# Fewer, larger first transfers: two row tiles of x at once, and eight k tiles of w_in in four pieces

## The chip, the cores and the metric

The kernel runs on one core of one Trainium2 chip. The metric is the device time of one execution in microseconds (us). The time given for a kernel is the median of several runs; details come from one profiled execution. The core's engines work side by side, each through its own list of instructions in order: TensorE (PE: matrix products, with PEld for its weight loads), VectorE (DVE), ScalarE (ACT), GpSimd (POOL), and SyncE (SP), which here issues every transfer. The transfers themselves are carried out by 16 DMA engines.

## What is computed

Two branches work on the same 2048 x 1024 input x, and a gate per row mixes them. Cut to what matters:

```python
def reference(A_x, A_wqkv, A_wo, B_x, B_w_in, B_w_sp, B_b_sp, B_w_out, gate_w):
    # a: attention, 32 heads of 32, each row looks at 8 rows (itself and 7 before, 2 apart)
    qkv = x @ wqkv; logits = q . k[idx] * Dh ** -0.5; o = softmax(logits) . v[idx]; a = o @ wo
    # b: a gated MLP with mixing over rows
    z = gelu(x @ w_in)                      # 2048 x 3584
    z1, z2 = z[:, :1792], layernorm(z[:, 1792:])
    b = (z1 * (w_sp @ z2 + b_sp)) @ w_out
    g = sigmoid((x * gate_w).sum(-1))
    return g * a + (1 - g) * b
```

x is the same tensor in both branches. All tensors are bf16; products add up in float32.

## The kernel before

Rows of x are cut into 16 row tiles of 128, and its 1024 columns into 8 k tiles of 128. Every product over x runs over the 8 k tiles, with 128 x 128 weights held in the array and up to 512 columns streamed past them. The product's time is set by the columns.

All data in the fast memory lie in one tile, `arena`, and the names are views of it: `xn` (two row tiles of x as they are stored, rows on partitions), `xT` (x transposed, k on partitions, which the products need), `w2` (the second half of w_in, by k tile, plus a column for the gate), `wg_slots` (weights of q, k and v), `z2`, and others. The profile calls all of them `arena`; `ps`, `pt` and `pw` are accumulator tiles.

The order of work is written by hand (`manual_schedule`, L393). TensorE's stages, in order:

1. `warm_up(6)` (L412): six products of zeros (L91), which wait for no transfer.
2. `z2_quad()` (L413): the first two row tiles, columns 0 to 1023 of the second half of w_in. Row tiles 0 and 1 come in untransposed as `xn`, and TensorE transposes them (16 instructions, L238). VectorE (L242) and ScalarE (L244) copy the results to `xT`, two k tiles an instruction. Then 32 products of 512 columns (L223) run with the k tile as the outer loop: for each k tile two row tiles times two column blocks, into four accumulators. So each k tile of w_in is needed for four products before the next one is needed.
3. Row tiles 2 to 15, columns 0 to 511 (`z2_tile(i, 0)`, L417). Their part of `xT` comes from transposing transfers (L403), one per row tile.
4. q, k and v, eight groups of heads (L431), while VectorE does the attention; then the rest of z2 (L452), z1 (L473), the mixing over rows (L487) and the output (L509, L513).

The edit lies in the transfers that SP issues for stages 1 and 2. In the order of its list: the two row tiles of x (L396), the eight k tiles of w_in, 128 x 1024 elements or 256 KB each (L398), the fourteen transposes of x (L403) with weights of the first head group in between (L198), and further weights.

A transfer's end is told by a counter. There are eight counters, used in turn, so a transfer may only be issued when the one eight before it has ended. In the compiled list before, transfers 1 to 8 wait for nothing; the seventh and eighth k tile (transfers 9 and 10) wait for the two x tiles, and the first transpose (transfer 11) waits for k tile 0 (transfer 3).

TensorE waits in the quad as follows: the first transpose of each row tile for that row tile's transfer, and the first product of each k tile for that k tile's transfer.

Of the kernel before, what the change touches and what calls it, by code (L numbers as in the profile page):

```python
# [16 lines left out]
KT = D // P  # L17
# [8 lines left out]
FH = 1792  # L26
NF = FH // P
ZC = 512
# [22 lines left out]
def kernel(  # L51
# [24 lines left out]
    def reg(off, n):  # L76
        return arena[:, off:off + n]
# [43 lines left out]
    xn = reg(A_OFF, 2 * D).rearrange("p (i d) -> p i d", i=2)  # L121
# [13 lines left out]
    w2 = reg(CD_OFF, KT * W2P).rearrange("p (k c) -> p k c", k=KT)  # L135
# [12 lines left out]
    x_v = x2.rearrange("(i q) d -> q i d", q=P)  # L148
# [3 lines left out]
    win_v = B_w_in.rearrange("(k p) c -> p k c", p=P)  # L152
    wsp_v = B_w_sp.rearrange("(a t) s -> a t s", t=P)
    wo_v = A_wo.rearrange("(g h d) n -> g h d n", g=NG, h=HG, d=DH)
    sync = nc.sync
# [236 lines left out]

    tc_order = ctx.enter_context(tc.manual_schedule())  # L393

    for i in range(2):
        sync.dma_start(xn[:, i, :], x_v[:, i, :])  # L396
    for kt in range(KT):
        sync.dma_start(w2[:, kt, 0:2 * ZC], win_v[:, kt, FH:FH + 2 * ZC])  # L398
    for i in range(2, 16):
        if i == 14:  # L400
            load_w(0, 3)
# [173 lines left out]
```

## Time and profile before

| | us |
|---|---|
| median of three runs | 716.58 (715.78 to 716.62) |
| the profiled execution | 716.54 |
| its span, first to last instruction | 714.7 |
| TensorE busy | 706.6 |
| VectorE busy | 414.0 |
| ScalarE busy | 251.3 |
| first product of the quad starts | 6.05 |

The span is what the profile covers; 1.8 us of the execution lie outside it. Busy times overlap, since the engines work side by side. The granted TensorE clock is 0.999 of full speed over the span. In the timeline a line gives the start, the duration or the stretch over which such instructions follow one another, the engine, the line of the kernel, what is written and read, how many, and in brackets the idle time before the first of them with what ended it. A transfer's line under SPq shows the time that SP takes to issue it, not the time that it takes.

### The profile page before, as it was taken

How to read it: one execution, taken by the hardware profiler on the slowest of the kernel's cores; microseconds unless marked ns; L12 is line 12 of the kernel's file. 1: busy time of each engine (PE TensorE's matmuls, PEld its weight loads, DVE VectorE, ACT ScalarE, POOL GpSimd, SP SyncE). 2: the span in 40 equal slices, each digit the busy share in tenths (PEclk: the TensorE clock that was granted, in tenths of full speed). 3: DMA queues.
4: the chain of work that ended last, by engine and by line, in shares of the span. 5: the costliest groups of instructions: out<-in, count | busy, mean ns of one | idle time of the engine just before them, and what ended most of it. 6: DMA issues, size and time to landing. Idle time of an engine off the chain costs nothing.

```text
span 714.7 us, 8897 instructions
## 1 busy us (share of the span) xinstructions
PE 706.6 (99%) x3577; PEld 402.0 (56%) x3628; DVE 414.0 (58%) x429; ACT 251.3 (35%) x483; POOL 11.0 (2%) x23
## 2 busy tenths in 40 slices
PE   8999999999999999999999999999999999999998
PEld 4488888888865554444444444444444444444444
DVE  0000989999999999999997999211222112221111
ACT  4444454445379894353521211111111111121111
POOL 1000000000000102000000000000000000000000
PEclk9999999999999999999999999999999999999999
DMA  9967776667781206954569580772400213002310
GB/s 238 191 149 220 165 200 170 167 133 193 202 237 66 85 1 181 253 184 137 173 196 293 213 174 2 220 146 59 133 1 0 55 49 119 1 1 59 60 45 29
DMA packets 176761, 92.93 MB, mean 130 GB/s; under 512 B 145104, under 2 KB 166992, under 8 KB 176208
## 3 DMA queue, kind: packets, MB, share of 16 engines
q1 hardware_dynamic: 176720, 92.36, 48.9%
q8 instruction: 28, 0.46, 0.3%
q14 instruction: 13, 0.11, 0.0%
HBM read 47.71 MB, written 28.38 MB: 106 GB/s over the span
## 4 chain that ended last, share of the span: by engine, by line
PE 98%; DMA 1%; issue 0%; SPq 0%; DVE 0%; DVEq 0%
PE ps L487 27%; PE ps L431 23%; PE ps L223 14%; PE ps L473 13%; PE psb L513 13%; PE psa L509 8%; DMA arena<-in_B_w_in_dram 1%; SPq L396 0%; DVE arena L517 0%; DVEq L517 0%
## 5 line engine op out<-in xcount | busy, mean ns | idle before, releaser
L487 PE MATMUL ps<-arena 128*128 128x512 bf16 x877 | 192.9, 379 | 1.0
L431 PE MATMUL ps<-arena 128*128 128x384 bf16 x1024 | 166.6, 326 | 0.0
L431 PEld LDWEIGHTS <-arena 128*128 128x128 bf16 x1024 | 147.6, 144 | 18.9
L487 PEld LDWEIGHTS <-arena 128*128 128x128 bf16 x896 | 87.7, 98 | 105.7
L513 PE MATMUL psb<-arena 128*128 128x512 bf16 (+1 forms) x455 | 101.3, 372 | 0.3
L223 PE MATMUL ps<-arena 128*128 128x512 bf16 (+1 forms) x501 | 96.7, 352 | 1.8 <-DMA arena<-in_B_w_in_dram 1.2
L517 DVE SCALAR_TENSOR_TENSOR arena<-psb,omg,arena 128x512 bf16<-128x512 f32 (+1 forms) x33 | 24.3, 735 | 125.4 <-PE psb L513 113.4
L473 PE MATMUL ps<-arena 128*128 128x512 bf16 x439 | 96.4, 379 | 0.5
L266 DVE TENSOR_TENSOR arena<-arena 128x8192 bf16<-128x8192 bf16 x16 | 70.8, 4423 | 43.1 <-DMA arena<-k_d 42.8
L434 ACT CAST arena<-ps 128x384 bf16<-128x384 f32 x128 | 60.5, 480 | 90.2 <-PE ps L431 87.2
L491 ACT CAST arena<-ps 128x512 bf16<-128x512 f32 x56 | 32.8, 586 | 163.4 <-PE ps L487 136.9
L269 DVE TENSOR_TENSOR arena<-arena 128x4096 bf16<-128x4096 bf16 (+1 forms) x64 | 77.7, 1214 | 1.9
L223 PEld LDWEIGHTS <-arena 128*128 128x128 bf16 x512 | 50.1, 98 | 48.0 <-issue 1.3
L513 PEld LDWEIGHTS <-arena 128*128 128x128 bf16 x462 | 45.2, 98 | 51.5
L473 PEld LDWEIGHTS <-arena 128*128 128x128 bf16 x448 | 43.9, 98 | 52.6
L299 DVE TENSOR_TENSOR arena<-arena,att_A 128x8192 bf16<-128x8192 bf16 x16 | 70.7, 4422 | 0.2
L492 DVE TENSOR_TENSOR arena<-arena 128x512 bf16<-128x512 bf16 x56 | 23.6, 422 | 77.9 <-ACT arena L491 77.9
L516 ACT ACTIVATE arena<-psa,g_s 128x512 f32<-128x512 f32 (+1 forms) x33 | 22.2, 674 | 122.3 <-PE psa L509 118.2
L509 PE MATMUL psa<-arena 128*128 128x512 bf16 (+1 forms) x259 | 60.2, 372 | 0.4
L475 ACT ACTIVATE arena<-ps 128x512 bf16<-128x512 f32 x56 | 33.1, 596 | 55.5 <-PE ps L473 49.3
L509 PEld LDWEIGHTS <-arena 128*128 128x128 bf16 x264 | 25.8, 98 | 29.7
L228 ACT ACTIVATE arena<-ps 128x512 bf16<-128x512 f32 (+1 forms) x64 | 34.2, 538 | 23.4 <-PE ps L223 22.1
(54 smaller groups left out, 254.0 us busy)
## 6 DMA issues: line engine op xcount, KB each, us to landing
arena<-k_d SPq DMA_DIRECT2D x8, 960.0 KB, 6.8
arena<-v_d SPq DMA_DIRECT2D x8, 960.0 KB, 5.4
z_d<-arena SPq DMA_DIRECT2D x14, 512.0 KB, 3.3
arena<-z_d SPq DMA_DIRECT2D x4, 1792.0 KB, 7.5
arena<-in_A_wqkv_dram SPq DMA_DIRECT2D x24, 256.0 KB, 4.6
arena<-in_B_w_in_dram SPq DMA_DIRECT2D x4, 1024.0 KB, 7.2
q_d<-arena SPq DMA_DIRECT2D x32, 128.0 KB, 2.1
k_d<-arena SPq DMA_DIRECT2D x32, 128.0 KB, 2.2
```

What stands on the lines that cost most here:

```text
L223: nc.tensor.matmul(ps[:, 0:N], xT[:, kt, i * P:(i + 1) * P], w2[:, kt, ZC * c:ZC * c + N], start=(kt == 0), stop=(kt == KT - 1))
L228: nc.scalar.activation(z2[:, i, ZC * c:ZC * c + n], ps[:, 0:n], ACT.Gelu_apprx_tanh, accum_out=s1[:, 4 * i + c:4 * i + c + 1])
L266: TT(prod.rearrange("p (w j c) -> p w j c", w=W, j=8, c=C), in0, in1, ALU.mult)
L269: return lambda: TT(pv[:, :, 0:half], pv[:, :, 0:half], pv[:, :, half:2 * half], ALU.add)
L299: TT(prod.rearrange("p (w j d h) -> p w j d h", w=W, j=8, d=DH, h=HG), in0, in1, ALU.mult)
L431: nc.tensor.matmul(ps[:, 0:3 * C].rearrange("p (t c) -> p t c", t=3), lhsT, wgt[:, 0:3, kt, :], start=(kt == 0), stop=(kt == KT - 1))
L434: nc.scalar.copy(st[:, j % 4, :], ps[:, 0:3 * C])
L473: nc.tensor.matmul(ps[:], w1[:, kt, (f % 4) * P:(f % 4 + 1) * P], xT[:, kt, 512 * c:512 * (c + 1)], start=(kt == 0), stop=(kt == KT - 1))
L475: nc.scalar.activation(z1s[:, c, :], ps[:], ACT.Gelu_apprx_tanh)
L487: nc.tensor.matmul(ps[:], z2[:, i, f * P:(f + 1) * P], wsp[:, i, :, :].rearrange("p a t -> p (a t)"), start=(i == 0), stop=(i == 15))
L509: nc.tensor.matmul(psa[:, 0:nw], oT[:, kt, :], wo_sb[:, kt, n0:n0 + nw], start=(kt == 0), stop=(kt == KT - 1))
L513: nc.tensor.matmul(psb[:, 0:nw], z1c[:, f, aa * P:(aa + 1) * P], w_out_sb[:, f, n0:n0 + nw], start=(f == 0), stop=(f == NF - 1))
```

## The change

The two row tiles of x become one transfer of 512 KB. The eight transfers of w_in's k tiles become four: k tile 0 (256 KB), k tiles 1 and 2 (512 KB), 3 and 4 (512 KB), and 5 to 7 (768 KB). The bytes, their places and the order in which they are asked for stay the same.

```diff
-    for i in range(2):
-        sync.dma_start(xn[:, i, :], x_v[:, i, :])
-    for kt in range(KT):
-        sync.dma_start(w2[:, kt, 0:2 * ZC], win_v[:, kt, FH:FH + 2 * ZC])
+    sync.dma_start(xn, x_v[:, 0:2, :])
+    for k0, k1 in ((0, 1), (1, 3), (3, 5), (5, 8)):
+        sync.dma_start(w2[:, k0:k1, 0:2 * ZC], win_v[:, k0:k1, FH:FH + 2 * ZC])
     for i in range(2, 16):
         if i == 14:
             load_w(0, 3)
```

In the compiled lists, the instructions of TensorE, VectorE, ScalarE and GpSimd are the same as before and in the same order. SP's list has five transfers fewer at its head. The transposes of row tiles 0 and 1 now wait for the one transfer of x. Products wait at k tiles 0, 1, 3 and 5. With five transfers ahead of them, the first three transposing transfers wait for no counter, and the fourth waits for x. All later lines of the program stand one line higher than before.

## The prediction

> **What bounds the kernel now.** I read the page first: busy time by engine, and the chain that ended last.
>
> ```profile
> span 714.7 us, 8897 instructions
> PE 706.6 (99%) x3577; PEld 402.0 (56%) x3628; DVE 414.0 (58%) x429; ACT 251.3 (35%) x483; POOL 11.0 (2%) x23
> PE 98%; DMA 1%; issue 0%; SPq 0%; DVE 0%; DVEq 0%
> ```
>
> TensorE is busy for 99% of the span and is 98% of the chain. It works through one fixed order, so whatever moves the start of its steady work moves the end by as much. The 1% that is DMA is what the edit touches. The chain of waits, cut to 0 to 40 us, says where that lies (start, length, what):
>
> ```profile
> 0.74 0.39 SPq L396
> 1.18 0.42 SPq L396
> 1.64 4.36 DMA arena<-in_B_w_in_dram
> 6.05 5.99 PE ps L223 x27
> ```
>
> SP issues the two x tiles at 0.74 and 1.18, then k tile 0 of w_in at 1.64. That lands 4.36 us later, at 6.00, and TensorE starts at 6.05. The timeline of the same stretch shows what fills the time till then:
>
> ```profile
> 1.19 2.74 PE L91 MATMUL pw<-warm 128*128 128x512 bf16 x6 [1.19 <-DVE warm L86]
> 3.72 1.12 PE L238 MATMUL pt<-ident,arena 128*128 128x128 bf16 x16
> 4.21 0.96 DVE L242 COPY arena<-pt 128x256 bf16<-128x256 bf16 x4 [3.08 <-PE pt L238]
> 4.54 1.20 ACT L244 COPY arena<-pt 128x256 bf16<-128x256 bf16 x4 [2.52 <-DVE arena L242]
> 6.02 18.66 SPq L403 DMA_TRANSPOSE arena<-in_A_x_dram  x12
> 6.05 24.12 PE L223 MATMUL ps<-arena 128*128 128x512 bf16 x109 [1.20 <-DMA arena<-in_B_w_in_dram]
> ```
>
> TensorE idles 1.20 us between the transposes (end 4.84) and the first product; that wait is all the edit can win. From 6.05 on no wait is printed. The pace comes from ScalarE's steady rows, which start 1.725 us apart (16.61, 18.33, 20.06) for eight products each: 0.2157 us a product. The quad has 32, four to a k tile, so a k tile is used up in 0.863 us and the quad ends at 6.05 + 32 x 0.2157 = 12.95.
>
> Next, the DMA view in narrow windows: the issue of k tile 0 (at 1.64), of k tiles 1, 4 and 5 (2.12, 3.54, 4.01), and the first two x transposes (6.02, 7.41). The last column is us from issue to landing.
>
> ```profile
> arena<-in_B_w_in_dram SPq DMA_DIRECT2D x1, 256.0 KB, 4.4
> arena<-in_B_w_in_dram SPq DMA_DIRECT2D x1, 256.0 KB, 4.6
> arena<-in_B_w_in_dram SPq DMA_DIRECT2D x1, 256.0 KB, 5.1
> arena<-in_B_w_in_dram SPq DMA_DIRECT2D x1, 256.0 KB, 5.3
> arena<-in_A_x_dram SPq DMA_TRANSPOSE x1, 5.7
> arena<-in_A_x_dram SPq DMA_TRANSPOSE x1, 5.2
> ```
>
> So the k tiles land at 6.0, 6.7, 7.3 (2.59 + 4.7, same view), ..., 8.6, 9.3, and the last at 5.1 + 5.5 = 10.6: one every 0.65 us, though issued every 0.475 us. The issue rate does not pace them. The table by stretches does (the last two columns: DMA share, GB/s):
>
> ```profile
> 2.20:2.40 0.20, 0.20 (x2) 0.00 (x0) 0.00 (x0) 0.00 (x0) 0.20 (x4) 1.00 0.44 174
> 3.00:4.00 1.00, 1.00 (x7) 0.44 (x6) 0.00 (x0) 0.00 (x0) 0.00 (x0) 1.00 1.10 272
> 5.00:6.00 1.00, 0.00 (x0) 0.00 (x0) 0.17 (x1) 0.98 (x4) 0.00 (x0) 1.00 0.96 369
> 8.00:9.00 1.00, 1.00 (x6) 0.48 (x5) 0.00 (x0) 0.00 (x0) 0.00 (x0) 1.00 1.06 408
> ```
>
> The DMA engines are full (share about 1) and move 370 to 408 GB/s; 262 KB at 400 GB/s is 0.65 us. Margins now: k tile 1 lands at 6.7 and is needed at 6.91; k tile 7 lands at 10.6, needed at 12.1.
>
> **The change part by part.** *x in one transfer.* One issue instead of two: k tile 0's issue moves from 1.64 to about 1.20 (the 0.44 us from 0.74 to 1.18). Bounds on the longer issue: 0.39 us (one x issue), and 0.61 us (a 256 KB weight load in shorter pieces, 1.21 us for two), so 1.17 to 1.40. The first x tile is now known landed only with the second, which today lands at 1.18 + 2.7 = 3.88. The transposes start at 3.72 today, because the six warm-up products end there; they would start at 3.75 to 3.95, up to 0.23 later. Behind them the copies on VectorE (end 5.17) and ScalarE (end 5.74) move as much. All of it lies under the wait for k tile 0, which lands at 5.54 or later by every bound below; the ScalarE copies are first needed at k tile 2. Without that cover it would cost 0.23 at most.
>
> *When k tile 0 lands.* Early bound: 4.36 us from issue, as today: 1.18 + 4.36 = 5.54. Late bound: no gain, 6.0, since the same 786 KB (both x tiles and k tile 0) pass through engines that are already full. The nearer row is the second: share 0.93 to 1.10 from 1.8 to 4.0 us, with one hole, 0.44 at 2.20 to 2.40, between the two x tiles. Filling it gives 0.2 x 0.56 = 0.11. I take 5.89; the first product is then at 5.94, a gain of 0.11.
>
> *k tiles 1 and 2 as one.* Here the gain is given back. K tile 1 may be used only when k tile 2 is there too. Late bound: today's 7.3 for k tile 2, or 7.45 if the longer first issue delays it; early bound: issued at 1.6 with the 4.7 us that k tile 2 takes today, 6.3. By bytes it is 7.3 - 0.11 = 7.19. Needed at 5.94 + 4 x 0.2157 = 6.80. TensorE stalls from 6.80 to 7.24 (0.05 from landing to start, as today), 0.44 us, and ends the quad at 7.24 + 28 x 0.2157 = 13.28: 0.33 us later than 12.95.
>
> *The other two.* K tiles 3 and 4 land at 8.6 - 0.1, needed at 7.24 + 8 x 0.2157 = 8.97. K tiles 5 to 7 land at 10.6 - 0.1 = 10.5, needed at 7.24 + 16 x 0.2157 = 10.69: no stall, with 0.19 to spare instead of 1.5.
>
> *SP's queue.* Ten issues become five. Today the first transpose waits for k tile 0 (it starts at 6.02, when that has landed; the wait view of SP gives 0.5 us) and now nothing holds the first three, so they are issued from about 3.1. Is that a threat to the last transfer? Today the first transpose is issued at 6.02, and the rate stays at 391 and 408 GB/s until 9.0 with landings still 0.65 apart; it lands at 11.7, after k tile 7's 10.6. So it queued behind. I cost it at nothing. Row tile 2 is needed at 13.28 and lands by 11.7 at the latest; the later transposes and weight loads stay in order behind it and only come earlier.
>
> One rule of the Trainium skill speaks for the edit: its page "DMA: Bandwidth & Descriptors" ("Rules for kernel authors") says to coalesce many small transfers, and its fit ("Anatomy of one DMA", given there for the GpSimd path) is about 2.0 us plus bytes over 436 GB/s. By that, as an estimate, the pair would be there 3.2 us after issue, at 4.8; nothing would stall, and the edit would gain most of the 1.20 us. The same section says that a completion is only signalled once the last byte has landed, which is what makes the pair late. The row decides: 256 KB takes 4.4 to 5.5 us here because the transfers queue, and fixed costs already overlap.
>
> **Sum.** -0.11 + 0.44 = +0.33 us. The profiled execution took 716.54 (714.7 span and 1.8 around it), which is the median of the runs (716.58) to 0.04. 716.54 + 0.33 = 716.87. All late bounds together (first product 6.05, pair at 7.45): 7.50 + 6.04 = 13.54, +0.59, 717.1. All early ones: first product at 5.59, the pair at 6.3 before its 6.45: -0.46, 716.1.
>
> **Rivals.** *The latency is counted from the issue*: then everything comes 0.44 earlier and the pair's stall shrinks to nothing: 716.1, at the utmost -0.46. For it: k tile 0 needs 2.1 us after x's second tile, with rates of only 123 to 246 GB/s at 3.8 to 4.6, where the engines are not full. Against: the 0.65 pace of the rest.
>
> *The transposes get in front of k tiles 5 to 7* (slower). Place: 8 to 11 us. Issued at 3.1 instead of 6.0, three could share the engines with the last transfer. One moves in 0.93 us (the second lands at 12.6, the first at 11.7). It decides once more than the 0.19 us to spare is taken. One in front: 0.33 + 0.93 - 0.19 = +1.07, 717.6; two: +2.0, 718.5; three: 719.5. Against: the undisturbed rate at 7 to 9 us.
>
> *The clock drops in the second pause* (slower). TensorE would pause twice within 2.4 us (1.1 and 0.44). It began at half pace: 0.427 a product from 1.19 to 3.83. One such stretch again, 2.64 us, has 6.2 products that lose 0.211 each: 1.3 us, 718.2 with the stall. Against: the 1.20 us pause today leaves the granted clock at 1.00 on both sides.
>
> **How the numbers follow.** Forecast 0.62, earlier by latency 0.20, transposes in front 0.08, clock 0.04, nothing named here 0.06. Forecast and first rival lie inside 0.2% (1.4 us), which is about what a measurement can tell from no change: the whole wait in question is 1.20 us. Same 0.82; slower 0.08 + 0.04 + 0.01 = 0.13; faster 0.05, all from the unnamed. Range: from 716.1 less 0.2 for the runs' own scatter (715.78 to 716.62) up to 718.2, which takes in the clock and one transpose in front. The likeliest case alone spans 716.1 to 717.1.
>
> **What will show it.** First product between 5.6 and 6.05; a second wait of TensorE on w_in, near 6.8, of about 0.44 us after four products; the quad's end near 13.3; first x transpose issued near 3.1, landing near 11.6; the rest of the chain unchanged. I am wrong if there is no second wait, if one appears near 10.7, or if the products after the pause start 0.427 apart.

## The result, and the profile after

The changed kernel takes 717.76 us (median of 21 runs, 716.18 to 718.26) against 716.48 us (21 runs, 715.78 to 716.90). The ratio is 1.0014, with a 95% interval of 1.0008 to 1.0020: it is slower, by 0.6 to 1.4 us, inside the 0.2% that the prediction called "same". The execution profiled took 716.63 us, 1.1 us under its kernel's median; more on that below.

The page of that execution, its busy times and its chain:

```profile
span 714.9 us, 8891 instructions
PE 707.4 (99%) x3577; PEld 402.5 (56%) x3628; DVE 414.1 (58%) x429; ACT 251.5 (35%) x483; POOL 11.0 (2%) x23
PE 99%; DMA 1%; issue 0%; DVE 0%; DVEq 0%
```

TensorE still does the same work, and this execution is only 0.1 us longer than the one profiled before (716.63 against 716.54). But the chain of waits from 0 to 40 us (start, length, what) takes another way:

```profile
0.74 3.60 DMA arena<-in_A_x_dram
4.38 1.82 PE pt L238 x16
6.20 5.92 PE ps L223 x27
```

Before, it ran through k tile 0 of w_in. Now it runs through x and the transposes, and w_in is not in it. The timeline of the changed kernel shows why:

```profile
3.24 21.21 SPq L402 DMA_TRANSPOSE arena<-in_A_x_dram  x12
4.38 1.82 PE L238 MATMUL pt<-ident,arena 128*128 128x128 bf16 x16 [0.45 <-DMA arena<-in_A_x_dram]
5.35 1.58 ACT L244 COPY arena<-pt 128x256 bf16<-128x256 bf16 x4 [3.34 <-DVE arena L242]
6.03 8.24 PE L223 MATMUL ps<-arena 128*128 128x512 bf16 x36
```

The transposes begin at 4.38 instead of 3.72 and take 1.82 us instead of 1.12, so the first product starts at 6.03, where it was before (6.05), though nothing of w_in holds it any more. The DMA view in narrow windows (x, k tile 0, the pair, k tiles 3 and 4, k tiles 5 to 7; KB, us from issue to landing):

```profile
arena<-in_A_x_dram SPq DMA_DIRECT2D x1, 512.0 KB, 3.6
arena<-in_B_w_in_dram SPq DMA_DIRECT2D x1, 256.0 KB, 3.7
arena<-in_B_w_in_dram SPq DMA_DIRECT2D x1, 512.0 KB, 5.2
arena<-in_B_w_in_dram SPq DMA_DIRECT2D x1, 512.0 KB, 6.1
arena<-in_B_w_in_dram SPq DMA_DIRECT2D x1, 768.0 KB, 7.5
```

With the issues at 0.74, 1.24, 1.74, 2.21 and 2.72 these land at 4.33, 4.97, 6.95, 8.28 and 10.26. K tile 0 is there a whole microsecond earlier than before, the pair two microseconds after it. The fifth product, the first that needs the pair, starts at 6.99 (6.91 before). Here, then, the pair costs next to nothing. In the median run something costs 1.1 us more than in this one, and one profile can't say what. That made the experiments necessary.

### The profile page after: what moved, and what is told of

It reads as the page before. It is cut to its first block, busy times and chain, and to the rows that moved or that the text cites. A ratio compares the mean times of both kernels' runs of the same rounds, so it can differ in the third digit from the quotient of the medians.

```text
span 714.9 us, 8891 instructions
## 1 busy us (share of the span) xinstructions
PE 707.4 (99%) x3577; PEld 402.5 (56%) x3628; DVE 414.1 (58%) x429; ACT 251.5 (35%) x483; POOL 11.0 (2%) x23
## 4 chain that ended last, share of the span: by engine, by line
PE 99%; DMA 1%; issue 0%; DVE 0%; DVEq 0%
PE ps L486 27%; PE ps L430 23%; PE ps L223 13%; PE ps L472 13%; PE psb L512 13%; PE psa L508 8%; DMA arena<-in_A_x_dram 1%; PE pt L238 0%; DVE arena L516 0%; DVEq L516 0%
```

## The experiments

Each kernel was run beside the kernel before on the same chip: 11 runs of each timed one, and 15 to 33 of before in each group. The differences below are between medians of one group; the ratio's interval stands with each.

Theory A was read off the profile above: TensorE pauses before its transposes, so it gets its full clock later (the trace has it granted from 5.99 us on, before from 3.85), and the median run is one where that came later still. Theory B is the prediction's: the pair of k tiles is late. The first four kernels tell them apart.

**x alone in one transfer.**

```diff
-    for i in range(2):
-        sync.dma_start(xn[:, i, :], x_v[:, i, :])
+    sync.dma_start(xn, x_v[:, 0:2, :])
```

> Only the two row tiles of x become one transfer; w_in keeps its eight. Theory A (clock): x is known landed only after the six warm-up products have ended (3.72 us), TensorE pauses before its transposes, and the full clock comes later than the 3.85 us of before; time as with the whole change, 717.0 to 718.0 us, and a profile with a pause near 3.7 and half-pace instructions after it. Theory B (k tiles 1 and 2 late as a pair): this part alone costs nothing, 715.9 to 716.7 us, the time of before.

Measured: 716.42 us against 716.52, ratio 0.9999 (0.9990 to 1.0008). This half of the change costs nothing that can be measured, though its profile has the pause:

```profile
4.25 1.28 PE L238 MATMUL pt<-ident,arena 128*128 128x128 bf16 x16 [0.32 <-DMA arena<-in_A_x_dram]
5.37 9.01 PE L223 MATMUL ps<-arena 128*128 128x512 bf16 x40
```

In this execution (715.89 us) k tile 0 landed at 4.90, products ran from 5.37 on, and there was no wait for w_in: eight single k tiles kept ahead.

**w_in alone in four transfers.**

```diff
-    for kt in range(KT):
-        sync.dma_start(w2[:, kt, 0:2 * ZC], win_v[:, kt, FH:FH + 2 * ZC])
+    for k0, k1 in ((0, 1), (1, 3), (3, 5), (5, 8)):
+        sync.dma_start(w2[:, k0:k1, 0:2 * ZC], win_v[:, k0:k1, FH:FH + 2 * ZC])
```

> Only w_in's eight transfers become four; x keeps its two. Theory A: no pause after the warm-up, the full clock comes near 3.85 us, time as before or up to 0.4 us less, 715.9 to 716.7 us. Theory B: the wait at k tile 1 is there, 716.8 to 717.8 us.

Measured: 717.75 against 716.52, ratio 1.0017 (1.0007 to 1.0027). The whole loss is in this half. Its timeline shows the wait at the pair, after four products:

```profile
5.91 1.02 PE L223 MATMUL ps<-arena 128*128 128x512 bf16 x4 [0.27 <-DMA arena<-in_B_w_in_dram]
7.65 6.63 PE L223 MATMUL ps<-arena 128*128 128x512 bf16 x29 [0.73 <-DMA arena<-in_B_w_in_dram]
```

**The whole change with more warm-up.**

```diff
-    warm_up(6)
+    warm_up(8)
```

> The whole change, with eight warm-up products instead of six, so that TensorE is busy until x has landed near 4.3 us. Theory A: no pause, the full clock comes near 3.85 us as before, time 715.6 to 716.6 us. Theory B: the two more products lie ahead of the quad and cannot help; 717.4 to 718.3 us, as the change without them.

Measured: 717.77 against 716.52, ratio 1.0018 (1.0009 to 1.0026). Theory A falls as the cause of the loss in the median. In the profile (717.22 us) it got all it asked for, transposes without a wait at the full clock, and the time won went into a longer wait for the pair:

```profile
4.27 1.06 PE L238 MATMUL pt<-ident,arena 128*128 128x128 bf16 x16
5.17 1.03 PE L223 MATMUL ps<-arena 128*128 128x512 bf16 x4
7.57 6.63 PE L223 MATMUL ps<-arena 128*128 128x512 bf16 x29 [1.37 <-DMA arena<-in_B_w_in_dram]
```

The first four products start 0.9 us earlier than before the change, and the fifth 0.7 later (7.57 against 6.91): an early first product is worth nothing if the fifth is late.

**The changed kernel again.**

> The changed kernel once more, for a second profile of it. Its median of 717.76 us is 1.1 us above the execution profiled first (716.63 us, full clock from 5.9 us). Theory A: in a profile of 717.6 us or more the full clock comes at 7.5 us or later, and the quad's first products start 0.427 us apart. Theory B: such a profile shows TensorE waiting about 1 us on w_in after four products, at the full clock.

Measured: 717.52 against 716.52, ratio 1.0017 (1.0008 to 1.0026). The profiled execution took 716.88, so neither expectation for one of 717.6 or more could be tested. Its timeline has no wait for w_in:

```profile
4.34 1.89 PE L238 MATMUL pt<-ident,arena 128*128 128x128 bf16 x16 [0.41 <-DMA arena<-in_A_x_dram]
6.02 8.27 PE L223 MATMUL ps<-arena 128*128 128x512 bf16 x35
```

Its first two products start 0.427 us apart (6.02 and 6.45), and the fifth at 7.22, although the pair had landed at 6.47. What held the fifth product back in this execution was not the pair but the half pace, which lasted until 6.69. So theory A's cost exists, some 0.3 us here (7.22 against 6.91), but it is not the loss of the median.

Meanwhile a theory C had come up: with fewer transfers ahead of it, the first transposing transfer goes out at 3.2 to 3.6 us instead of 6.0 and might disturb w_in's. The next kernels separate it from B. In their diffs the loop over pieces stands in place of the one over eight single k tiles.

**The pair alone.**

```diff
+    for k0, k1 in ((0, 1), (1, 3), (3, 4), (4, 5), (5, 6), (6, 7), (7, 8)):
```

> x in two transfers, w_in in seven: k tiles 1 and 2 as one, all others alone. The first transposing transfer is issued only near 5.1 us, as nine transfers lie ahead of it. Theory B (the pair lands late): the loss is here, 717.2 to 718.2 us, with a wait of TensorE after four products in the profile. Theory C (transposing transfers that are issued from 3.2 to 3.6 us instead of 6.0 disturb the transfers of w_in): no loss, 716.0 to 716.8 us.

Measured: 717.49 against 716.41, ratio 1.0011 (1.0001 to 1.0021). The pair alone costs +1.08 us, with the transposing transfer issued at 5.36. The profiled execution (717.64 us) is an example:

```profile
arena<-in_B_w_in_dram SPq DMA_DIRECT2D x1, 512.0 KB, 5.8
5.43 1.74 PE L223 MATMUL ps<-arena 128*128 128x512 bf16 x4
7.98 6.20 PE L223 MATMUL ps<-arena 128*128 128x512 bf16 x27 [0.82 <-DMA arena<-in_B_w_in_dram]
```

K tile 0 had landed at 5.27, and the first four products were done issuing by 7.13 although they ran at half pace (1.74 us for four, against 1.03 above). The pair, issued at 2.11, landed at 7.94.

**Everything merged but the pair.** Two kernels, without and with x in one transfer:

```diff
+    for k0, k1 in ((0, 1), (1, 2), (2, 3), (3, 5), (5, 8)):
```

> x in two transfers, w_in in five: k tiles 0, 1 and 2 alone, 3 and 4 as one, 5 to 7 as one. The first transposing transfer is issued near 4.1 us, almost 2 us earlier than before. Theory B: no loss, 715.9 to 716.8 us. Theory C: the loss stays, 717.0 to 718.2 us.

> The whole change but for the pair: x in one transfer, w_in as k tiles 0, 1 and 2 alone, 3 and 4 as one, 5 to 7 as one. Theory B: 715.8 to 716.7 us, as with x alone in one transfer (716.42). Theory C: 717.0 to 718.2 us, as the whole change.

Measured: 717.20 against 716.41, ratio 1.0008 (0.9998 to 1.0018), and 716.87 against 716.41, ratio 1.0005 (0.9996 to 1.0014). The first lies in C's range (717.0 to 718.2), the second between B's and C's: less is lost than with the pair, but something seems to be. The medians are +0.79 and +0.46, with intervals that include no loss.

**x in one transfer with eight warm-up products.**

> x in one transfer, w_in in its eight, eight warm-up products instead of six. In the profile of x in one transfer alone k tile 0 landed at 4.90 us instead of 6.01, but the transposes began at 4.25 instead of 3.72, some of them at half pace. Theory A in its smaller form (the pause before the transposes gives away part of what the earlier k tile 0 wins): the transposes run at the full clock, the first product starts at 5.1 to 5.4 us, 715.2 to 716.1 us. If the pause costs nothing: 716.4 us, as without the two products.

Measured: 716.62 against 716.41, ratio 0.9998 (0.9989 to 1.0007). No gain. In the profile the transposes started at 4.58, behind eight warm-up products that all ran at half pace, and the first product at 6.07: in that execution the longer warm-up itself was in the way.

**Only such pairs as the arithmetic allows.** Without and with x in one transfer:

```diff
+    for k0, k1 in ((0, 1), (1, 2), (2, 3), (3, 4), (4, 6), (6, 8)):
```

> x in two transfers; w_in in six: k tiles 0 to 3 alone, 4 and 5 as one, 6 and 7 as one. The first transposing transfer goes out near 4.6 us, 1.4 us before its time of before. Theory B (a piece is late when its last k tile lands after its first is needed): k tile n lands at about 6.0 + 0.66 n and is needed at 6.05 + 0.86 n, so a pair starting at 4 lands at 9.3 and is needed at 9.5, and one at 6 lands at 10.6, needed at 11.2: no loss, 715.9 to 716.7 us. Theory C (early transposing transfers disturb w_in): a loss of about 0.7 us as in the kernel with k tiles 3 and 4, and 5 to 7, merged (717.2): 717.0 to 717.6 us.

> The same six pieces of w_in with x in one transfer; the first transposing transfer goes out near 4.2 us. Theory B: as x in one transfer alone (716.42 us), 715.8 to 716.7 us. Theory C: 716.8 to 717.6 us.

Measured: 716.85 against 716.36, ratio 1.0009 (1.0000 to 1.0018), and 716.69 against 716.36, ratio 1.0006 (0.9997 to 1.0015). The second is inside B's range, the first 0.15 us above it. The first's profiled execution (717.28 us) shows the loss; the first line is from its chain of waits, the second from its timeline:

```profile
3.54 6.56 DMA arena<-in_B_w_in_dram
10.14 4.04 PE L223 MATMUL ps<-arena 128*128 128x512 bf16 x17 [0.42 <-DMA arena<-in_B_w_in_dram]
```

The pair of k tiles 4 and 5 was expected at 9.3 and landed at 10.10. The transfer's parts on the 16 engines are counted one by one in the trace: fifteen were done by 9.22, the last at 10.10. A piece is done when its slowest part is. This is not peculiar to merged pieces: before the change, the last part of each of k tiles 0 to 6 came 0.36 to 0.39 us after the fifteenth. But here the lag was 0.88. B's arithmetic with single landings was too kind.

**The changed kernel a third time.**

> The changed kernel a third time, for its profile: the two profiled executions so far took 716.63 and 716.88 us, below the median. Theory B: the end follows the start of the fifth product of the quad (k tile 1), time = start + 709.6 us within 0.2 us, whatever that start is; an execution of 717.5 us or more has TensorE waiting for the pair until about 7.9 us. Theory C: the pair is there by 7.3 us and the loss lies behind it, in the wait for k tiles 3 or 5.

Measured: 717.10 us in this one execution. The waits (us in total, how many, the longest) and the timeline:

```profile
PE ps L223 <- DMA arena<-in_B_w_in_dram: 1.0, 1, 1.0
5.44 1.03 PE L223 MATMUL ps<-arena 128*128 128x512 bf16 x4
7.46 6.85 PE L223 MATMUL ps<-arena 128*128 128x512 bf16 x30 [0.99 <-DMA arena<-in_B_w_in_dram]
```

The only wait for w_in is for the pair (1.0 us); it landed at 7.42. The sum of B holds: fifth product plus 709.6 gives 7.46 + 709.6 = 717.1. The same sum fits other profiled executions in which no later product waits for w_in, whatever held the fifth back: the first of this kernel (6.99, 716.63), the second (7.22, 716.88), eight warm-up products (7.57, 717.22), the pair alone (7.98, 717.64), and before (6.91, 716.54), each within 0.1 us; w_in alone in four transfers (7.65, 717.40) lies 0.15 us above it. C's expectation, a loss behind the pair, is not seen; what B expected of an execution of 717.5 us or more stays untested, since none was profiled.

**The later pieces, with the transposing transfers held back.**

```diff
+    for k0, k1 in ((0, 1), (1, 2), (2, 3), (3, 5), (5, 8)):
...
+    for r in range(3):
+        sync.dma_start(junk[:, 64 * r:64 * r + 64], x2[0:P, 64 * r:64 * r + 64])
```

> x in two transfers, w_in in five pieces (k tiles 0, 1, 2 alone, 3 and 4, 5 to 7), which lost 0.8 us (717.2), and behind them three small loads of x, 16 KB each, whose data nothing uses. They put the first transposing transfer, which went out at 4.05 us without them, back to about 6.0 us as before the change, since it now waits for k tile 0. Theory C (early transposing transfers disturb the last pieces): the loss goes, 716.2 to 716.7 us. Theory B (the large last pieces are late by themselves): 716.9 to 717.5 us.

Measured: 717.20 against 716.39, ratio 1.0010 (1.0001 to 1.0019), as without the small loads (717.20). The timeline of the profiled execution (716.86 us):

```profile
5.84 9.02 SPq L405 DMA_TRANSPOSE arena<-in_A_x_dram  x5
5.74 2.75 PE L223 MATMUL ps<-arena 128*128 128x512 bf16 x12 [0.86 <-DMA arena<-in_B_w_in_dram]
8.65 5.59 PE L223 MATMUL ps<-arena 128*128 128x512 bf16 x24 [0.16 <-DMA arena<-in_B_w_in_dram]
```

The first transposing transfer goes out at 5.84, and the products still stop twice: at k tile 3 (its piece landed at 8.60; undisturbed, the product would have started at 8.33 instead of 8.65) and at k tile 5 (piece landed at 10.59, product at 10.63 instead of 10.37). Theory C falls for these pieces. For the pair, x alone speaks against it too: its first transposing transfer went out at 5.12, earlier than in the pair alone (5.36), and nothing was lost.

## Why the prediction was right, and where it was off

The time (717.76) lies in the range, but above the 717.1 that the likeliest case reached. It is inside because the range made room for a lower clock in the second pause and for one transpose in front of the last piece, and neither happened: that part is luck. By its number alone the rival with one transpose in front (717.6) was nearer than the forecast (716.87). The mechanism of the forecast is the one that the experiments show, a loss at the pair: x alone -0.10 us (no measurable gain), the pair alone +1.08, all of w_in's merging +1.23, the whole change +1.28 and +1.00 in its two timed groups. The second wait on w_in, without which the prediction called itself wrong, is printed in one of the three profiles of the changed kernel (0.99 us in the third), and in those of w_in alone in four (0.73), eight warm-up products (1.37) and the pair alone (0.82). What failed is the size, +0.33, and several steps under it. Point by point:

- *k tile 0 lands at 5.89, at the earliest 5.54.* It landed at 4.97, 4.97 and 4.88 in the three profiles of the changed kernel. The early bound took the 4.36 us of before as the least that such a transfer needs; it took 3.6 to 3.7. The argument that full engines leave no gain was wrong, and the rows of before don't bear it out: besides the hole at 2.20 they have shares of 0.88, 0.83, 0.58 and 0.66 from 3.8 to 4.6, with k tile 0 still on its way. That slow stretch, 123 to 246 GB/s, was not there after the change (406 and 408 GB/s at 3 to 5 us).
- *x lands by 3.95 and the transposes hide under k tile 0.* x landed at 4.33, 4.29 and 4.13. The cover was gone with k tile 0 early; the prediction had priced that at 0.23 us at most. In the first profile the transposes ended 1.36 us later than before (6.20 against 4.84): 0.66 for the later start, and 0.70 because they ran slower, which the prediction had put at nothing. There they end the wait instead, and the first product starts at 6.03 all the same: the gain of 0.11 that was booked was nothing there, and 0.6 in the third (5.44).
- *The pair lands at 7.19 and costs 0.44 us.* It landed at 6.95, 6.47 and 7.42; the fifth product started at 6.99, 7.22 and 7.46 against 7.24 predicted. The profiled executions (716.63, 716.88, 717.10) lie around the forecast of 716.87, but the second meets it by luck: there the half pace delayed the fifth product, not the pair. For the median the forecast is wrong: by the sum above, 717.7 us means a fifth product near 8.1, 0.9 us later than predicted, if nothing behind it waits. This is the term that was mis-sized, the stall at the pair. The pair alone shows such an execution (start at 7.98, landing at 7.94, past the 7.45 that was given as the late bound); of the changed kernel itself no profile shows one. The late bound took the landing of k tile 2 alone; one piece of 512 KB can land later than its second half did by itself.
- *K tiles 3 and 4 and 5 to 7 cost nothing, the last with 0.19 to spare.* That holds behind the pair: no wait for them in the three profiles, with 0.15 to spare in the third (landed at 10.76, needed at 7.46 + 16 x 0.2157 = 10.91). Without the pair they cost something of their own, 0.46 to 0.81 us in three medians, of which the interval excludes zero in one.
- *The early transposing transfers cost nothing.* Right as far as tested: held back, with the pair split, they changed nothing, and in the changed kernel the first landed at 11.27 in the first profile, behind the last piece (10.26), as argued.
- *The Trainium skill's rule on coalescing and its fit* (page "DMA: Bandwidth & Descriptors", "Rules for kernel authors" and "Anatomy of one DMA"), by which, as an estimate, the edit would have gained most of 1.20 us: not borne out. The pair took 4.7 to 5.8 us from issue, against an estimate of 3.2 by the page's fit. The DMA engines' share was 1.05 and 1.08 at 3 to 5 us in the first profile, so it probably queued behind other bytes; and that k tile 1 could not be used before k tile 2 is what cost.
- *The rivals.* That latency counts from the issue does not hold: k tile 0 came 1.0 us earlier, more than the 0.44 that this gives, and the pair between 0.9 us earlier and 0.1 later than k tile 2 had come before (7.33). The clock did not drop in the pause at the pair (the products behind it are 0.22 us apart in the third profile). What the prediction lacks is that the full clock can come later from the start, which cost some 0.3 us in the second profile. No wait for the last piece shows in any of the three.

What stays open: why timed executions of the changed kernel (median of all 33: 717.7) are slower than the three profiled ones, while before the change both agree (x alone has it in small, 715.89 profiled and a median of 716.42); why k tile 0 landed 1.0 us earlier than before when it was issued only 0.4 us earlier; and why one part of a piece lags (0.7 us in the first profile's pair: fifteen parts by 6.27, the last at 6.95). No version beat the kernel before beyond its interval; x alone in one transfer (ratio 0.9999) is its equal.

## What to carry to other kernels

Merge transfers only where the consumer has more slack than the merged piece adds: here one k tile landed every 0.65 us and was used up every 0.86, so slack grows by only 0.2 us a tile, and a piece of two at the second place costs 1.1 us. Keep the first pieces small when they feed an engine that is about to run without a break; large pieces, if any, belong behind, and even there they gained nothing here. And test the slack with some reserve, since a transfer ends with its slowest part: a pair that fitted with 0.2 us to spare on paper was late in a profiled run.

## What the runs showed of the hardware

The full TensorE clock comes at a time that differs between executions with the same instructions ahead of it. The sixteen transposes, started at 3.72 behind the same six products, took 1.12 us before the change. In the pair alone, the timeline has 1.91 us for them:

```profile
3.72 1.91 PE L238 MATMUL pt<-ident,arena 128*128 128x128 bf16 x16
```

The first products after them were still 0.427 us apart, up to 6.71. The traces have the full clock granted from 3.85 us on before the change and from 6.86 on in the pair alone, 2.7 and 5.7 us after the first warm-up product (1.19). The Trainium skill's page "TensorE: Matmul & The Clock Gate" (Part 1) has the clock set by a window of 3.4 us that runs freely against the program, and a spread of 3.0 us is no wider than that window. The same part puts the change at around 4 us into the work, within 0.5 us from run to run; these runs differ by more than that, and the measurement decides. Warm-up products help in some executions and not in others, as the two kernels with eight of them show: transposes at full pace from 4.27 in one, at half pace from 4.58 in the other.

With x as one transfer, k tile 0 landed between 4.81 and 4.97 us in all eight profiles, and with x as two between 5.27 and 6.01 in six, although only 0.4 us of that is the earlier issue. Why the rest came is not shown.
